# Semaphores between GpSimd and VectorE, 22 products of zeros, and a new written-out order in a windowed-attention and highway kernel

## The chip, the cores and the metric

The kernel runs on one core of one Trainium2 chip. The metric is the device time of one launch in microseconds (us). The kernel before was run three times: 172.64, 172.2 and 172.1 us, a median of 172.2. One more execution was recorded by the profiler; it is the source of every profile line.

## What is computed

Attention with a sliding window and a distance bias, over 8 batches, 8 heads, 576 positions and head size 64; its output is the input x of a highway layer of 4608 tokens by 512.

```python
scores = scale * np.matmul(q, k.transpose(0, 1, 3, 2))
bias = slopes[:, None, None] * (-np.abs(rel).astype(np.float32))[None, :, :]
mask = (rel >= 0) & (rel < window)                 # window = 128
scores = np.where(mask, scores + bias[None], -1000000000.0)
attn = softmax(scores); attn_out = np.matmul(attn, v)
H = np.maximum(x @ w_h, 0.0)
T = 1.0 / (1.0 + np.exp(-(x @ w_t + b_t)))
out = T * H + (1.0 - T) * x
```

## The kernel before, in words

**Stages.** Each batch has four stages of 128 positions; the last 64 positions of two batches make one more stage, so there are 36 of these "blocks". The attention weights are exp(score) times a table which holds exp(bias) inside the window and zero outside it. A column of ones beside v gives the sums. The gate is taken from tanh: T = 0.5 + 0.5 tanh(z / 2), and the output is T (H - x) + x.

**Order by hand.** The framework schedules nothing. A string, ORDER, lists steps of one letter and a two-digit number, and each engine gets its instructions in that order; a semaphore is waited for wherever data or a buffer demands it. The string is the output of a planner outside the kernel. The string BANKS gives, in the same order, the PSUM bank that each product takes. The letters that the text uses, with line and engine:

- L, V, W: loads of q or k (L128), of v (L134), of the weights wH and wT (L138) and the bias bT (L142). All are issued by GpSimd. L00 to L03 are batch 0's q and k, L04 to L07 batch 1's; V00 is batch 0's v. W00 is wH, W01 wT. Eight semaphores serve these loads in turn, so a load also waits until the eighth load before it has landed. There are two sets of q/k tiles: L08 overwrites what L00 brought, after the transpose T00.
- R, P, Q, A: clearing of tiles by VectorE (L152 to L170). S, r, k: the table, by GpSimd (L179, L181), VectorE (L185 to L189) and ScalarE (L194, L198). B: a copy of the bias to all partitions, issued by SyncE.
- T: transpose of a q or k tile, VectorE, L211. Four per batch are needed before its first scores.
- s: scores, TensorE, L239 and L249. e: exp, ScalarE, L263. m: product with the table ("the mask"), VectorE, L270.
- p, y, Y: weights times v, TensorE, L303 (Y drains TensorE first). n: normalisation, VectorE, a reciprocal (L312) and a product (L313).
- x, c: transpose on TensorE (L322) and copy on ScalarE (L327). h: product with w_h, TensorE, L332. z: product with w_t, TensorE, L359 and, for the bias, L363, or b, a copy of the bias by ScalarE (L350).
- u: ScalarE's relu (L342), followed by v, VectorE's H - x (L346); or U: both in one, VectorE (L338).
- a: tanh, ScalarE, L367. Then 0.5 + 0.5 t: t on ScalarE (L372) or D on VectorE (L374).
- the gate's product: G on GpSimd or g on VectorE (both L380). The sum with x: o on GpSimd or O on VectorE (both L385). d: store, issued by SyncE (L391, L395).

**VectorE's operations with two operands in SBUF** are m (L270), v (L346), g (L380) and O (L385); D (L374) has one, in 16 bits, input and output in SBUF. The text calls these five "with lock", because the change treats them alike. T, n and U are not among them: T has one operand, and the others read PSUM.

**Where GpSimd stands.** G and o wait for their data alone; the letter's place in ORDER decides what is before and behind it in GpSimd's own queue, but not how it stands against VectorE. In ORDER the list has, for example, "... m12 m13 m14 ... m15 ... G09 ..." : G09 is written behind the mask m15, but no semaphore says so.

The string before begins: R00 L00 L01 Q00 L02 L03 P00 S00 V00 r00 W00 T00 k00 W01 T01 W02 L04 T02 L05 L06 and so on.

Of the kernel before, what the change touches and what calls it, by code (L numbers as in the profile page):

```python
# [15 lines left out]
ORDER = (
    "R00L00L01Q00L02L03P00S00V00r00W00T00k00W01T01W02L04T02L05L06L07T03A00s00s01e00e01s02m00L"
    "08e02s03m01e03p00m02V01Y00p01n00Y01p02n01x00Y02c00x01n02h00L09c01m03x02z00U00c02T04h01a0"
    "0v00p03z01T05D00Y03G00a01T06z02t01o00h02T07a02L10d00U02u01s04B00n03G01e04T08s05L11e05s06"
    "L12m04L13e06x03m05p04Y04v02c03n04s07p05m06e07x04h03D02T09G02Y05c04p06T10L14U03Y06V02h04b"  # L20
    "03n05z03v03n06L15x05z04a03m07c05x06z05a04T11o01c06h05u04L16a05d01T12s08b06h06U05D05e08D0"
    "3v05z06T13G03p07U06s09m08L17a06Y07e09V03p08n07Y08n08x07s10L18c07m09x08e10h07T14o03p09c08"
    "p10u07Y09o02t04Y10n09b08h08G05t06d02n10d03x09z07c09v06L19U08m10L20z08a07L21g04s11v08a08g"
    "06D07x10T15o06e11z09O04V04h09g07c10d04s12D08m11U09z10e12T16o05h10a09G08s13a10d05u10d06p1"
    "1e13p12D10Y11v09o07Y12n11s14n12G10e14x11d07T17x12L22c11s15D09c12m12h11e15m13h12m14p13U11"
    "p14m15Y13b11p15Y14U12z11n13G09z12n14a11L23v11x13T18o08x14c13p16y15t11Y16v12L24d08a12z13n"
    "15o09c14b14n16x15h13a13G11d09T19t13h14c15o11T20z14U14L25h15D12u13a14L26s16D14V05T21U15z1"
    "5e16v14x16O10p17L27a15s17m16d10c16Y17d11e17D15h16G12n17p18b16u16G14s18T22Y18e18x17o12z16"
    "n18c17G13s19d12T23a16h17e19V06D16m17z17m18U17s20a17v15p19m19e20p20Y19Y20G15n19t17s21n20p"
    "21o13e21Y21T24x18o14x19d13c18s22n21c19h18L28e22d14m20h19m21U18s23v17b19x20T25G17e23z18T2"  # L30
    "6o15z19c20T27p22G16x21a18d15h20c21u19a19L29h21m22U20L30z20m23U21t19y22p23a20o17n22p24Y23"
    "p25n23Y24L31Y25G19n24p26x22x23n25c22z21o19c23T28x24o16y26a21h22T29c24b22V07d16x25h23d17D"
    "18c25n26t20z22v18U23v20s24u22a22h24e24g18D21v21z23g20v23b24O18s25a23D22z24d18m24U24d19e2"
    "5x26g22h25T30o20z25t23u25d20c26m25s26a24h26a25T31o22e26z26D24U26m26s27a26p27g21e27Y27g23"
    "p28o21n27Y28n28x27d21s28d22c27v24p29e28D25x28m27h27c28Y29m28U27s29g24h28b27v26e29n29o24z"
    "27u28p30t26g25s30m29a27Y30e30x29G26n30z28c29o23s31a28z29e31D28d23m30d24x30g28h29v27c30D2"
    "7m31p31a29p32Y31h30b30n31o26U29z30U30O25x31y32v29a30d25p33d26c31n32p34Y33t29p35D30v30x32"
    "g27h31c32n33G30h32O28z31g29U32u31o27b32y34a31y35n34x33o30d27z32c33d28n35x34z33a32O29t31D"
    "32d29x35c34g31h33d30v32g32z34O31U33a33O32d31h34c35v33d32a34D33z35g33t34u34h35O33a35g34d3"
    "3D35U35O34v35d34g35O35d35"  # L40
)
BANKS = (
    "4040640376304602504074065402435403401240240124176242014234024034012406123421036240124120"
    "4143142042014034021467106204673623104013401241042034023423042341024601520467636272034503"
)


# [22 lines left out]
def kernel(  # L70
# [74 lines left out]
    def pads(i):  # L145
        for g in range(NG):
            for w in "qk":
                nc.vector.memset(TR[i, g, w][:, S:SQ, :], 0.0)

    def clear(step):  # L150
        if step == "R":
            nc.vector.memset(ident[:], 1.0)  # L152
            nc.vector.memset(ones0[:], 0.0)
            nc.vector.memset(ones0[0:1, :], 1.0)
            nc.vector.memset(bT[:], 0.0)
            nc.vector.memset(VA[0][:, :, D : D + 1], 1.0)
            pads(0)
        elif step == "P":
            for p in PB:
                nc.vector.memset(p[:, :, 0:64], 0.0)  # L160
                nc.vector.memset(p[:, :, 256:320], 0.0)
                nc.vector.memset(p[:, :, 512:576], 0.0)
        elif step == "Q":
            for p in PE3:
                nc.vector.memset(p[:, :, 0:64], 0.0)
            nc.vector.memset(MK3[:, :, :, 192:256], 0.0)
# [36 lines left out]
    def additive():  # L203
        for h in range(NH):
            for g in range(NG):
                nc.gpsimd.tensor_scalar(
                    out=MA[:, h, g, :], in0=rel[:], scalar1=-slopes[4 * g + h] / scale,
                    scalar2=None, op0=ALU.mult)

    def tr(w, b, g):  # L210
        nc.vector.transpose(  # L211
            out=TR[b % 2, g, w][:, 0:S].rearrange("p s e -> p (s e)").bitcast(U32).rearrange(
                "p (s t) -> p t s", t=NT),
            in_=LD[b % 2, g, w][:].bitcast(U32).rearrange("p (t i) -> p t i", i=32))
# [52 lines left out]

    def mask(b, s):
        p = pview(b, s)
        nc.vector.tensor_tensor(out=p, in0=p, in1=(MK3 if s == 3 else MK)[:], op=ALU.mult)  # L270
# [46 lines left out]
    XP, XT, PA, PZ, TT, UU, OT = {}, {}, {}, {}, {}, {}, {}  # L317
# [25 lines left out]

    def sub_x(b, s):
        uu = UU[b, s][:]
        nc.vector.tensor_tensor(out=uu, in0=uu, in1=X[b, s][:], op=ALU.subtract)  # L346
# [22 lines left out]
    def to_gate(b, s, on):  # L369
        tt = TT[b, s]  # L370
        if on == "t":
            nc.scalar.activation(out=tt[:], in_=tt[:], func=ACTF.Copy, bias=0.5, scale=0.5)  # L372
        else:
            nc.vector.tensor_scalar(out=tt[:], in0=tt[:], scalar1=0.5, scalar2=0.5,  # L374
                                    op0=ALU.mult, op1=ALU.add)

    def gate(b, s, on):
        eng = nc.vector if on == "g" else nc.gpsimd
        uu = UU[b, s][:]
        eng.tensor_tensor(out=uu, in0=uu, in1=TT.pop((b, s))[:], op=ALU.mult)  # L380

    def add_x(b, s, on):
        eng = nc.gpsimd if on == "o" else nc.vector
        ot = OT[b, s] = ft.tile([P, DM], F32, name="ot")
        eng.tensor_tensor(out=ot[:], in0=UU.pop((b, s))[:], in1=X[b, s][:], op=ALU.add)  # L385
# [57 lines left out]
```

## Time and profile before

| what | value |
|---|---|
| median of three runs | 172.2 us (172.1 to 172.64) |
| the profiled execution, its own time | 172.49 us |
| its span, first to last instruction | 170.5 us |
| mean granted TensorE clock | 0.924 |
| PE / DVE / ACT / POOL busy | 135.1 / 152.8 / 119.3 / 94.0 us |
| GpSimd tensor operations | 18 gates (L380) and 25 sums (L385) |
| loads | 15.21 MB through GpSimd's queue, 81.9% of 16 engines' span |

In the lines to come, PE is TensorE, PEld its weight loads, DVE VectorE, ACT ScalarE, POOL GpSimd and SP SyncE. A group's line ends with busy us, mean ns of one, and idle time before it with what ended that. A timeline row begins with start and duration in us and covers several instructions where it ends in "x3". The slices cut the span into 40 parts and give the busy share in tenths. The granted clock is 1 at full speed.

### The profile page before, as it was taken

How to read it: one execution, taken by the hardware profiler on the slowest of the kernel's cores; microseconds unless marked ns; L12 is line 12 of the kernel's file. 1: busy time of each engine (PE TensorE's matmuls, PEld its weight loads, DVE VectorE, ACT ScalarE, POOL GpSimd, SP SyncE). 2: the span in 40 equal slices, each digit the busy share in tenths (PEclk: the TensorE clock that was granted, in tenths of full speed). 3: DMA queues.
4: the chain of work that ended last, by engine and by line, in shares of the span. 5: the costliest groups of instructions: out<-in, count | busy, mean ns of one | idle time of the engine just before them, and what ended most of it. 6: DMA issues, size and time to landing. Idle time of an engine off the chain costs nothing.

```text
span 170.5 us, 6188 instructions
## 1 busy us (share of the span) xinstructions
PE 135.1 (79%) x2696; PEld 73.8 (43%) x2696; DVE 152.8 (90%) x268; ACT 119.3 (70%) x172; POOL 94.0 (55%) x93
## 2 busy tenths in 40 slices
PE   0016999679998996899992899995999999999940
PEld 0014744434454443545450447443645555565410
DVE  7995699796889999999999987999999998899990
ACT  3199656952698796674883479991599999975740
POOL 7951508457089488690978619299609217318000
PEclk9999999755999999659999579999999999999997
DMA  3999999999989999968199891739495030333452
GB/s 55 198 157 198 211 205 160 217 203 148 190 156 137 234 230 136 262 93 188 18 158 169 218 123 62 139 79 186 107 159 171 25 127 4 125 110 139 161 212 62
DMA packets 48106, 25.30 MB, mean 148 GB/s; under 512 B 38224, under 2 KB 39248, under 8 KB 48080
## 3 DMA queue, kind: packets, MB, share of 16 engines
q0 software_dynamic: 42688, 15.21, 81.9%
q1 hardware_dynamic: 5392, 9.70, 15.9%
q8 instruction: 21, 0.34, 0.8%
q14 instruction: 5, 0.04, 0.1%
HBM read 30.67 MB, written 9.44 MB: 235 GB/s over the span
## 4 chain that ended last, share of the span: by engine, by line
DVE 43%; PE 24%; POOL 12%; issue 12%; ACT 6%; DVEq 0%; POOLq 0%; ACTq 0%
DVE p L270 7%; PE ps L303 6%; PE ps L359 6%; PE ps L332 6%; DVE x L313 5%; POOL ot L385 5%; DVE tt L374 4%; ACT p L263 4%; POOL uu L380 4%; DVE ot L385 3%; PE ps L322 3%; DVE uu L380 3%; PE ps L239 3%; DVE uu L346 2%; DVE uu L338 2%
## 5 line engine op out<-in xcount | busy, mean ns | idle before, releaser
L380 POOL TENSOR_TENSOR uu<-uu,tt 128x512 bf16<-128x512 bf16 x18 | 25.7, 1430 | 38.9 <-DVE tt L374 17.6
L385 POOL TENSOR_TENSOR ot<-uu,x 128x512 f32<-128x512 bf16 x25 | 33.4, 1346 | 15.9 <-DVE uu L380 12.2
L332 PE MATMUL ps<-wH,xt 128*128 128x512 bf16 x144 | 40.3, 412 | 0.0
L263 ACT ACTIVATE p<-ps 128x1536 bf16<-128x1536 f32 x24 | 34.5, 1455 | 7.4 <-PE ps L239 7.4
L359 PE MATMUL ps<-wT,xt 128*128 128x512 bf16 x144 | 37.8, 387 | 0.2 <-DVE x L313 0.2
L303 PE MATMUL ps<-va,p 64*128 64x65 bf16 x768 | 25.4, 204 | 9.5 <-DVE x L313 4.0
L270 DVE TENSOR_TENSOR p<-p,mk 128x1536 bf16<-128x1536 bf16 x24 | 28.7, 1211 | 2.5 <-ACT p L263 2.5
L367 ACT ACTIVATE tt<-ps 128x512 f16<-128x512 f32 x36 | 21.4, 602 | 11.6 <-PE ps L359 7.2
L327 ACT COPY xt<-ps 128x512 bf16<-128x512 bf16 x36 | 20.8, 586 | 10.0 <-PE ps L322 9.6
L303 PEld LDWEIGHTS <-p 64*128 64x128 bf16 x768 | 18.9, 102 | 19.7 <-issue 15.5
L313 DVE TENSOR_TENSOR x<-ps,rd 128x512 bf16<-128x512 f32 x36 | 24.9, 691 | 1.5
L332 PEld LDWEIGHTS <-xt 128*128 128x128 bf16 x144 | 13.4, 104 | 15.1 <-issue 3.9
L359 PEld LDWEIGHTS <-xt 128*128 128x128 bf16 x144 | 13.2, 100 | 14.1 <-issue 1.8
L342 ACT ACTIVATE uu<-ps 128x512 bf16<-128x512 f32 x24 | 14.4, 602 | 5.8 <-PE ps L332 5.4
L322 PE MATMUL ps<-ident,x 128*128 128x128 bf16 x144 | 15.2, 235 | 3.2 <-issue 1.2
L263 ACT ACTIVATE r<-ps 128x2048 bf16<-128x2048 f32 x8 | 15.0, 1876 | 2.1 <-PE ps L249 1.9
L239 PE MATMUL ps<-tr00q,tr00k 32*64 32x192 bf16 x256 | 7.1, 294 | 11.8 <-DVE tr00q L211 10.4
L134 POOL DMA_DIRECT2D va<-in_v_dram x8 | 15.0, 1873 | 1.4 <-DMA wH<-in_moe_w_h_dram 1.4
L374 DVE TENSOR_SCALAR tt<-tt 128x512 f16<-128x512 f16 x23 | 11.9, 521 | 2.4 <-ACT tt L367 2.4
L322 PEld LDWEIGHTS <-x 128*128 128x128 bf16 x144 | 9.7, 103 | 9.3 <-DVE x L313 3.7
L270 DVE TENSOR_TENSOR r<-r,mk 128x2048 bf16<-128x2048 bf16 x8 | 11.6, 1455 | 0.1
L346 DVE TENSOR_TENSOR uu<-uu,x 128x512 bf16<-128x512 bf16 x24 | 10.6, 446 | 0.7 <-ACT uu L342 0.7
(75 smaller groups left out, 192.1 us busy)
## 6 DMA issues: line engine op xcount, KB each, us to landing
out_dram<-ot SPq DMA_DIRECT2D x32, 256.0 KB, 2.5
va<-in_v_dram POOLq DMA_DIRECT2D x8, 576.0 KB, 9.9
ld00k<-in_k_dram POOLq DMA_DIRECT2D x4, 288.0 KB, 8.2
ld00q<-in_q_dram POOLq DMA_DIRECT2D x4, 288.0 KB, 5.0
ld01k<-in_k_dram POOLq DMA_DIRECT2D x4, 288.0 KB, 6.6
ld01q<-in_q_dram POOLq DMA_DIRECT2D x4, 288.0 KB, 7.2
ld10k<-in_k_dram POOLq DMA_DIRECT2D x4, 288.0 KB, 7.9
ld10q<-in_q_dram POOLq DMA_DIRECT2D x4, 288.0 KB, 8.9
```

The lines of the kernel that those rows point to most:

```text
L263: nc.scalar.activation(out=pview(b, s), in_=SC.pop((b, s))[:, :, 0:n].rearrange("p h (g n) -> p h g n", g=NG), func=ACTF.Exp, scale=scale)
L270: nc.vector.tensor_tensor(out=p, in0=p, in1=(MK3 if s == 3 else MK)[:], op=ALU.mult)
L303: mm = nc.tensor.matmul(out=av[o : o + m, par, j * (D + 1) : (j + 1) * (D + 1)], lhsT=PT[bb, st][rows, h, c : c + m], rhs=VA[bb][rows, at ...
L313: nc.vector.tensor_tensor(out=x[:].rearrange("p (i r d) -> p r i d", i=NH, r=2), in0=av[:, :, :, 0:D], in1=rd[:].to_broadcast([P, 2, NH, D ...
L322: nc.tensor.transpose(out=pt[:, c * P : (c + 1) * P], in_=X[b, s][:, c * P : (c + 1) * P], identity=ident[:])
L327: nc.scalar.copy(out=xt[:].rearrange("p c n -> p (c n)"), in_=XP.pop((b, s)))
L332: nc.tensor.matmul(out=pa, lhsT=XT[b, s][:, c, :], rhs=wH[:, c, :], start=c == 0, stop=c == NC - 1)
L359: nc.tensor.matmul(out=pz, lhsT=xt[:, c, :], rhs=wT[:, c, :], start=c == 0 and not given, stop=c == NC - 1 and given, skip_group_check=given)
L367: nc.scalar.activation(out=tt[:], in_=PZ.pop((b, s)), func=ACTF.Tanh, scale=0.5)
L374: nc.vector.tensor_scalar(out=tt[:], in0=tt[:], scalar1=0.5, scalar2=0.5, op0=ALU.mult, op1=ALU.add)
L380: eng.tensor_tensor(out=uu, in0=uu, in1=TT.pop((b, s))[:], op=ALU.mult)
L385: eng.tensor_tensor(out=ot[:], in0=UU.pop((b, s))[:], in1=X[b, s][:], op=ALU.add)
```

## The change

- GpSimd's G and o get one more semaphore: each waits for the last VectorE operation with lock that stands ahead of it in ORDER (`alone` notes it, `between` adds the wait). Loads that GpSimd issues get none.
- VectorE clears one more tile (J), and TensorE multiplies it with itself 22 times (K) ahead of its first scores, into a bank that the scores overwrite later.
- ORDER and BANKS are new. Counted by letter, VectorE's D goes from 23 to 19 and ScalarE's t from 13 to 17; GpSimd's G from 18 to 15 and VectorE's g from 18 to 21; GpSimd's o from 25 to 24 and VectorE's O from 11 to 12; the drains Y from 30 to 28. All other counts are the same.
- A helper that this kernel doesn't call (`additive`; ADD is empty) moves to ScalarE.

The new ORDER begins: R00 L00 B00 L01 P00 L02 L03 L04 S00 J00 Q00 K00 L05 A00 L06 L07 r00 V00 T00 k00 W00 T01 L08 T02 V01 T03 T04 s00 L09 s01 e00 W01 T05. Batch 1's loads now stand ahead of V00 and of both weights, and its four transposes T04 to T07 ahead of the first mask.

```diff
+SPIN = 22
 ORDER = (
-    "R00L00L01Q00L02L03P00S00V00r00W00T00k00W01T01W02L04T02L05L06L07T03A00s00s01e00e01s02m00L"
...
+    "R00L00B00L01P00L02L03L04S00J00Q00K00L05A00L06L07r00V00T00k00W00T01L08T02V01T03T04s00L09s"
...
+    spin = cp.tile([P, DM], BF16, name="spin")
     PS = pp.tile([P, 8, 512], F32, name="ps")
+
+    paired = [None]
+
+    def alone(ins):
+        paired[0] = ins.ins
+
+    def between(ins):
+        if paired[0] is not None:
+            tc.add_manual_dep(
+                ins.ins, paired[0].name,
+                mybir.DependencyInfo(mybir.DependencyClass.Sync, mybir.DependencyReason.DATA),
+                reason="starts behind VectorE's last operation with two SBUF operands")
...
+        if step == "J":
+            nc.vector.memset(spin[:], 0.0)
...
+    def warm():
+        ps = take(1)[:, 0, :]
+        for _ in range(SPIN):
+            nc.tensor.matmul(out=ps, lhsT=spin[:, 0:P], rhs=spin[:], start=True, stop=True)
...
-        nc.vector.tensor_tensor(out=p, in0=p, in1=(MK3 if s == 3 else MK)[:], op=ALU.mult)
+        alone(nc.vector.tensor_tensor(out=p, in0=p, in1=(MK3 if s == 3 else MK)[:], op=ALU.mult))
...
-        nc.vector.tensor_tensor(out=uu, in0=uu, in1=X[b, s][:], op=ALU.subtract)
+        alone(nc.vector.tensor_tensor(out=uu, in0=uu, in1=X[b, s][:], op=ALU.subtract))
...
-            nc.vector.tensor_scalar(out=tt[:], in0=tt[:], scalar1=0.5, scalar2=0.5,
-                                    op0=ALU.mult, op1=ALU.add)
+            alone(nc.vector.tensor_scalar(out=tt[:], in0=tt[:], scalar1=0.5, scalar2=0.5,
+                                          op0=ALU.mult, op1=ALU.add))
...
-        eng = nc.vector if on == "g" else nc.gpsimd
+        eng, note = (nc.vector, alone) if on == "g" else (nc.gpsimd, between)
         uu = UU[b, s][:]
-        eng.tensor_tensor(out=uu, in0=uu, in1=TT.pop((b, s))[:], op=ALU.mult)
+        note(eng.tensor_tensor(out=uu, in0=uu, in1=TT.pop((b, s))[:], op=ALU.mult))
...
-        eng = nc.gpsimd if on == "o" else nc.vector
+        eng, note = (nc.gpsimd, between) if on == "o" else (nc.vector, alone)
         ot = OT[b, s] = ft.tile([P, DM], F32, name="ot")
-        eng.tensor_tensor(out=ot[:], in0=UU.pop((b, s))[:], in1=X[b, s][:], op=ALU.add)
+        note(eng.tensor_tensor(out=ot[:], in0=UU.pop((b, s))[:], in1=X[b, s][:], op=ALU.add))
```

More of the change, by code (lines that the diff above doesn't have):

```diff
@@ L16 @@
 ORDER = (
-    "R00L00L01Q00L02L03P00S00V00r00W00T00k00W01T01W02L04T02L05L06L07T03A00s00s01e00e01s02m00L"
[L18 to L40, printed above, removed]
+    "R00L00B00L01P00L02L03L04S00J00Q00K00L05A00L06L07r00V00T00k00W00T01L08T02V01T03T04s00L09s"
@@ new lines @@
+    "01e00W01T05e01s02W02T06e02s03L10T07e03m00s04m01e04s05m02L11e05m03p00p01Y00m04p02n00Y01L1"
+    "2x00n01Y02c00p03L13n02x01h00c01T08s06U00y03e06x02n03h01m05x03c02L14s07c03u01h02e07m06L15"
+    "h03T09U02p04m07p05U03p06Y04Y05n04V02z00v00n05x04p07T10L16c04y06Y07a00z01n06b03t00n07z02a"
+    "01G00T11x05x06L17c05h04T12a02L18s08c06o00u04z03e08v02d00z04v03D01b06T13G01s09a03h05a04T1"
+    "4L19e09h06o01T15z05U05L20d01U06v05V03D04s10D02a05m08p08e10z06m09L21x07Y08D05c07g02s11D03"
+    "a06n08G04h07e11T16G05x08z07u07L22c08m10s12a07p09e12v06Y09o02p10n09Y10o04s13n10d02p11e13T"
@@ new lines @@
+    "17x09G03x10Y11T18c09s14o03c10h08e14n11L23h09d03D06d04V04m11U08s15b08x11m12e15z08m13z09m1"
+    "4U09z10a08T19o05c11p12a09p13m15L24d05Y12t09L25h10b11v08t08n12G06h11a10u10t07z11U11O06p14"
+    "a11G07y13d06p15n13Y14p16Y15o07n14Y16x12n15p17G08c12d07x13n16Y17c13x14o08x15n17c14h12c15v"
+    "09h13t10d08D11g09U12s16T20o09b14z12e16u13L26d09h14T21V05a12s17U14T22z13e17L27m16z14V06a1"
+    "3v11s18g10a14v12p18D13e18x16v14z15m17c16g13s19m18a15h15e19T23o10y18h16n18L28d10U15L29s20"
+    "g11L30T24b16p19o11e20Y19z16n19o13d11t14x17T25p20c17L31Y20a16u16s21G14t12x18n20e21z17V07D"
@@ new lines @@
+    "15g12x19v15c18x20m19h17a17c19z18m20U17c20s22T26o12b19h18e22T27o14d12z19d13U18s23m21d14a1"
+    "8h19m22e23z20u19D18a19D16p21m23p22a20p23Y21t17Y22n21t20h20g15p24n22U20o15y23Y24n23p25x21"
+    "G16d15Y25c21n24x22z21c22v17T28o16t19p26a21x23n25G17h21d16c23b22x24g19x25c24y26o19z22U21n"
+    "26c25h22v18t21g18a22x26O17z23c26v20d17v21s24u22G21h23e24T29o18h24T30U23s25a23d18h25m24b2"
+    "4d19U24z24D22e25u25g20z25v23D23a24T31o20s26a25h26e26m25d20z26D24U26m26s27a26g22p27e27v24"
+    "Y27o22p28n27Y28o21n28x27s28c27p29m27e28d21x28d22h27D25c28s29m28Y29e29g23h28n29o23U27s30u"
@@ L41 @@
+    "28d23b27p30g24x29m29e30z27O24Y30c29s31d24n30a27z28e31v26D27g25x30v27z29m30a28g27c30h29m3"
+    "1p31p32U29p33o27Y31b30Y32n31a29z30t29D26D28x31n32G26p34a30y33c31Y34n33G28t30p35x32n34h30"
+    "c32O26x33x34c33y35v29h31O25c34U30g29d25z31d26v30b32d27n35G30z32a31u31x35t31O29h32c35O28a"
+    "32h33g31d28U32O30d29z33U33v32d30O31t32z34a33v33d31g32t33h34O32a34g33d32h35t34o33u34z35U3"
+    "5g34d33v35O34a35d34D35g35O35d35"
 )
 BANKS = (
-    "4040640376304602504074065402435403401240240124176242014234024034012406123421036240124120"
@@ L44 @@
-    "4143142042014034021467106204673623104013401241042034023423042341024601520467636272034503"
+    "4404040642160504570672407624750460460547047074506406540540567124076026504536506740504670"
+    "6706404067540607405642064621305436541705604570450646046706074606752306234130354701726326"
+    "0"
 )
@@ L150, in clear @@
     def clear(step):
-        if step == "R":
+        if step == "J":
+            nc.vector.memset(spin[:], 0.0)
+        elif step == "R":
             nc.vector.memset(ident[:], 1.0)
@@ L205, in additive @@
             for g in range(NG):
-                nc.gpsimd.tensor_scalar(
-                    out=MA[:, h, g, :], in0=rel[:], scalar1=-slopes[4 * g + h] / scale,
-                    scalar2=None, op0=ALU.mult)
+                nc.scalar.activation(out=MA[:, h, g, :], in_=rel[:], func=ACTF.Copy,
+                                     scale=-slopes[4 * g + h] / scale)
     def tr(w, b, g):
@@ L405 @@
                 continue
-            if step in "RPQA":
+            if step == "K":
+                warm()
+                continue
+            if step in "JRPQA":
                 clear(step)
```

## The prediction

> **What bounds the kernel now.** I read the page first: busy shares, the slices and the chain.
>
> ```profile
> PE 135.1 (79%) x2696; PEld 73.8 (43%) x2696; DVE 152.8 (90%) x268; ACT 119.3 (70%) x172; POOL 94.0 (55%) x93
> DVE  7995699796889999999999987999999998899990
> PEclk9999999755999999659999579999999999999997
> DVE 43%; PE 24%; POOL 12%; issue 12%; ACT 6%; DVEq 0%; POOLq 0%; ACTq 0%
> ```
>
> VectorE (DVE) is busy 152.8 of 170.5 us, almost without a hole from the fourth tenth on, and holds 43% of the chain. TensorE (PE) comes second. Its clock is about halved in three places (the 5s and the 6). So a microsecond less on VectorE shortens the run until TensorE is late.
>
> How much of the 152.8 us is work? The answers by source line give minimum/median/maximum, the groups by form give means:
>
> ```profile
> L270 DVE TENSOR_TENSOR p<-p,mk x24: 930/955/2861, 14.6 to 146.6; 128x1536 bf16<-128x1536 bf16 x24
> L270 DVE TENSOR_TENSOR r<-r,mk x8: 1211/1218/2171, 22.0 to 148.3; 128x2048 bf16<-128x2048 bf16 x8
> L374 DVE TENSOR_SCALAR tt<-tt x23: 277/288/1500, 25.7 to 163.8; 128x512 f16<-128x512 f16 x23
> L346 DVE TENSOR_TENSOR uu<-uu,x x24: 403/418/868, 24.3 to 164.6; 128x512 bf16<-128x512 bf16 x24
> L380 DVE TENSOR_TENSOR uu<-uu,tt x18: 405/418/1375, 59.0 to 165.1; 128x512 bf16<-128x512 bf16 x18
> L385 DVE TENSOR_TENSOR ot<-uu,x x11: 658/684/799, 61.3 to 165.6; 128x512 f32<-128x512 bf16 x11
> ...
> L270 DVE TENSOR_TENSOR p<-p,mk 128x1536 bf16<-128x1536 bf16 x24 | 28.7, 1211 | 2.5 <-ACT p L263 2.5
> L374 DVE TENSOR_SCALAR tt<-tt 128x512 f16<-128x512 f16 x23 | 11.9, 521 | 2.4 <-ACT tt L367 2.4
> L270 DVE TENSOR_TENSOR r<-r,mk 128x2048 bf16<-128x2048 bf16 x8 | 11.6, 1455 | 0.1
> L346 DVE TENSOR_TENSOR uu<-uu,x 128x512 bf16<-128x512 bf16 x24 | 10.6, 446 | 0.7 <-ACT uu L342 0.7
> L380 DVE TENSOR_TENSOR uu<-uu,tt 128x512 bf16<-128x512 bf16 x18 | 9.4, 524 | 0.1
> ```
>
> Mean minus median, times count: 24 x 256 ns = 6.1; 8 x 237 = 1.9; 23 x 233 = 5.4; 24 x 28 = 0.7; 18 x 106 = 1.9. Together **16.1 us** in which VectorE stood inside an instruction. GpSimd (POOL) beside it shows why:
>
> ```profile
> 71.52 1.78 POOL L380 TENSOR_TENSOR uu<-uu,tt 128x512 bf16<-128x512 bf16 x1 [1.67 <-DVE tt L374]
> 73.86 1.26 POOL L385 TENSOR_TENSOR ot<-uu,x 128x512 f32<-128x512 bf16 x1
> 75.67 1.28 POOL L385 TENSOR_TENSOR ot<-uu,x 128x512 f32<-128x512 bf16 x1
> ...
> 71.35 4.59 DVE L270 TENSOR_TENSOR p<-p,mk 128x1536 bf16<-128x1536 bf16 x3
> 75.86 2.17 DVE L270 TENSOR_TENSOR r<-r,mk 128x2048 bf16<-128x2048 bf16 x1
> ```
>
> Three masks took 4.59 us (three medians: 2.87) and the fourth 2.17 (median 1.22), while three GpSimd operations ran. In the order list these three (G09, o08, o09) stand behind m15, v11 and v12, that is, behind all four masks. They had their data and started up to 6.5 us ahead of their place. Going through all lengthened VectorE operations in the timeline, I find 17 beside GpSimd tensor operations, and in each the GpSimd operation stood later in the list than it ran; those that ran on time lengthened nothing. Two more stood beside a load that GpSimd was issuing, and end with it:
>
> ```profile
> 84.77 1.85 POOL L134 DMA_DIRECT2D va<-in_v_dram  x1
> 85.23 1.50 DVE L374 TENSOR_SCALAR tt<-tt 128x512 f16<-128x512 f16 x1
> ...
> 61.31 1.87 POOL L134 DMA_DIRECT2D va<-in_v_dram  x1
> 61.94 1.38 DVE L380 TENSOR_TENSOR uu<-uu,tt 128x512 bf16<-128x512 bf16 x1
> ```
>
> They cost 1.21 + 0.96 = 2.2 us; the tensor operations therefore 16.1 - 2.2 = **13.9 us**.
>
> **The change, part by part.** The profiled run took 172.49 us, 0.3 above the median of 172.2; its span is 170.5. I sum against 172.5.
>
> *The waits: -13.9.* A GpSimd tensor operation can no longer start ahead of the VectorE operation before it in the list, so the early kind goes. What is left: walking the new list, I add up the VectorE operations without lock that follow each of the 39 GpSimd operations, against about 1.15 us of one. In 34 cases these cover it (two transposes, or two normalisations); five are short by 0.06, 0.31, 0.06, 0.31 and 0.55 us: **+1.3**. A GpSimd operation can also come late, where several stand behind one VectorE operation or behind an issue. One such case costs up to a whole one (0.95 us for a mask above). None to five are possible; I take one: **+1.0**. Behind a waiting operation in GpSimd's queue stand the next loads, and whoever transposes them. GpSimd has room: 94.0 us busy, and it loses four operations.
>
> *Issues are not covered.* In the new list V03 stands right before two L374 operations, V04 right behind one, V07 right before one. Zero to three meetings at 1.2 us against 2.2 us now: -2.2 to +1.4, taken as 0.
>
> The Trainium skill, "SBUF — State Buffer", section "SBUF: two separate sides", calls the shared port pair an exclusive lock which the one that starts first keeps for the whole instruction. The 17 cases agree. It adds that two SBUF inputs alone meet only a GpSimd operation that reads SBUF; by that the 1.38 us at 61.94 should not have been, so here the row decides.
>
> *Work moved between engines: +1.0.* VectorE gives four L374 to ScalarE (-4 x 0.29), takes three gates (3 x 0.42) and one sum (0.68) from GpSimd, and clears one more tile (0.27, as the row below). ScalarE gets 4 x 0.63 = 2.5 us on 119.3, which its idle time takes.
>
> ```profile
> L166 DVE MEMSET mk<- 128x256 uint32 x1 | 0.3, 272 | 0.0
> L372 ACT ACTIVATE tt<-tt 128x512 f16<-128x512 f16 x13 | 8.2, 631 | 0.1
> 10.36 0.55 PE L239 MATMUL ps<-tr00q,tr00k 32*64 32x192 bf16 x16 [10.36 <-DVE tr00q L211]
> 96.69 1.71 PE ps L359 x4
> 100.94 0.86 PE ps L359 x4
> ```
>
> *The 22 products: 0.* TensorE idles for its first 10.36 us. At the slow clock four products of 512 columns take 1.71 us, so 22 take 9.4, at the fast clock (0.86) 4.7. They can start once their tile is cleared, some 4.5 us in, and end between 9.2 and 13.9. The scores need four transposes, done at about 12.5 now. So the products are covered, or late by 1.4 at most. Their worth is a fast clock for the first scores; but those are paced by the loads, below, so between 0 and -1.4, and I take 0.
>
> *The order at the front: -3.0.* It moves the four q/k loads of batch 1 ahead of V00 and the weights. From issue to landing:
>
> ```profile
> ld01q<-in_q_dram POOLq DMA_DIRECT2D x1, 288.0 KB, 6.9
> ld11q<-in_q_dram POOLq DMA_DIRECT2D x1, 288.0 KB, 15.1
> va<-in_v_dram POOLq DMA_DIRECT2D x1, 576.0 KB, 10.6
> wT<-in_moe_w_t_dram POOLq DMA_DIRECT2D x1, 512.0 KB, 12.3
> ...
> 3.09 0.55 POOL L128 DMA_DIRECT2D ld01q<-in_q_dram  x1
> 4.68 1.96 POOL L134 DMA_DIRECT2D va<-in_v_dram  x1
> 7.38 0.76 POOL L138 DMA_DIRECT2D wT<-in_moe_w_t_dram  x1
> 22.74 1.03 PE L359 MATMUL ps<-wT,xt 128*128 128x512 bf16 x4
> ```
>
> Now the fourth load lands at 10.0, V00 at 15.3, wT at 19.7: they land one behind the other. Put in the new order at these gaps (q/k 1.45, v 5, a weight 2.2), V00 lands at about 21 and wT, now behind V00, wH, L08, V01 and L09, at about 34. The first gate product moves from 22.7 to 34: +11.3 at worst. Against it, VectorE gets four transposes and two masks early:
>
> ```profile
> 13.00:45.00 32.00, 26.82 (x528) 15.68 (x513) 25.93 (x41) 20.64 (x24) 14.29 (x16) 0.84 1.47 189
> 45.00:100.00 55.00, 46.87 (x950) 24.65 (x948) 52.49 (x73) 39.21 (x54) 37.85 (x33) 0.88 1.22 169
> 100.00:165.00 65.00, 60.33 (x1197) 32.53 (x1195) 61.64 (x110) 53.31 (x77) 32.37 (x25) 1.00 0.55 117
> ```
>
> (Columns: window, length, busy of PE, PEld, DVE, ACT, POOL, clock, DMA.) VectorE idles 6.1 us between 13 and 45, the most that can be won. Bounds -6.1 and +11.3; I take half the idle time, since VectorE is the engine that ends last and it has work without wT.
>
> *TensorE gives back: +2.5.* Behind 100 us TensorE is busy 60.3 of 65.0, so hardly more than 4.7 us can go there. Of the 13.9 us about 5 lie there (the masks at 113 and 116 alone are 2.9). I let half pass.
>
> *The clock: -1.4.* Between 45 and 100 it averages 0.88. The L359 group at 96.69 took 1.71 us and the one behind it 0.86; two such groups on the chain cost some 1.4 us, and with VectorE quicker TensorE waits less there.
>
> Sum: 172.5 - 13.9 + 1.3 + 1.0 + 1.0 - 3.0 + 2.5 - 1.4 = 160.0; against the median, 0.3 less: **159.7**.
>
> **The rivals.**
>
> *TensorE becomes the bound, 167.* If nothing passes behind 100 us and half between 45 and 100, the waits win 13.9 - 5 - 4.5 = 4.4, less 1.0 for moved work, and the front -1.5: 167.3. For it: 60.3 of 65. Against it: chain and slices show VectorE.
>
> *The front starves the gates, 174: slower.* If all behind the first gate product follows wT and moves by 11.3 us, against 13.9 - 1.3 - 1.0 - 1.0 - 2.5 + 1.4 = 9.5 won, the run takes 174.0 after the 0.3. It decides if the sixth L359 group, at 44.9 now, comes after 54. Against it: now three of the six run before 28 and the next only at 42.5, so there is slack behind the first.
>
> *The collisions stay, 171.* If GpSimd mostly comes late, it meets the next locked operation instead: 172.5 + 1.0 - 3.0 = 170.5, or about unchanged.
>
> *The clock falls again.* In 13 to 45 it averaged 0.84 although TensorE was busy 26.8 of 32. With V00 at 21 the scores after the products run thin, and a second slow stretch of ten microseconds at half speed costs at most 5: 164.7 when it all reaches the end. The Trainium skill, "TensorE: Matmul & The Clock Gate", section "Part 1: The HAM clock gate", says an idle window of about 3.4 us brings the half clock back. By that rule, the products' worth would be gone before V00 lands.
>
> **How the numbers follow.** Forecast (150.8 to 165): 0.50; the falling clock, 164.7: 0.10. TensorE: 0.14. Collisions stay: 0.08, half of it within 0.3%, about what a measurement of this kernel can tell from no change. Front: 0.18, slower. So faster 0.78, same 0.04, slower 0.18. The low end takes all 6.1 us at the front and lets TensorE pass all: 172.5 - 13.9 + 1.0 - 6.1 - 1.4 - 0.3 = 151.8, less 1.0 of issue meetings: 150.8. The high end, 173.5, takes in all but the worse part of the front.
>
> **What would show it.** Right: VectorE means at their medians (masks near 0.96, L374 near 0.29), VectorE busy near 138, GpSimd operations starting right behind VectorE ones, V00's first use near 21, the first L359 group near 34 but the sixth before 46. Wrong: lengthened masks beside GpSimd operations, now late ones; the sixth L359 behind 54; TensorE with gaps and a clock under 0.8 up to 45; loads queued behind waiting GpSimd operations and transposes idle for them.

## The result and the profile after

| | before | after |
|---|---|---|
| median, all runs | 172.15 us (171.47 to 172.64, 4 runs) | 162.16 us (161.11 to 162.92, 4 runs) |
| ratio after / before | | 0.9418 [0.9353, 0.9484] |
| profiled execution, own time / span | 172.49 / 170.5 us | 162.92 / 161.1 us |
| mean granted TensorE clock | 0.924 | 0.939 |

The change is 10.0 us faster, where 12.5 was forecast (159.7). Ratios here and below leave out a kernel's slow executions (over 1.5% above its fastest), so they differ a little from the quotients of the medians given. The page of after: busy times, VectorE's slices, the clock, the chain.

```profile
PE 135.3 (84%) x2718; PEld 73.7 (46%) x2718; DVE 140.5 (87%) x269; ACT 121.2 (75%) x176; POOL 79.6 (49%) x89
DVE  7899956698999999757899999899899999889980
PEclk9998555999999997799999999999999999999996
PE 68%; ACT 13%; DVE 10%; issue 5%
```

VectorE is 12.3 us less busy, TensorE the same. The chain now lies on TensorE (68%, was 24%) instead of VectorE (10%, was 43%). A slowed clock shows in two places only (the 5s and the 7s), but the first lies early, in the fifth to seventh slice. The clock row counts the time ahead of the trace's first record of the clock as full speed, and it isn't: before the change, matmuls run at the slow clock up to about 21.9 us (sixteen scores in 0.55 us where they take 0.38 later, rows under old_products), though the row of before has 9s there.

The answers by line of after, masks and D (minimum/median/maximum):

```profile
L291 DVE TENSOR_TENSOR p<-p,mk x24: 931/946/1086, 17.7 to 136.4; 128x1536 bf16<-128x1536 bf16 x24
L291 DVE TENSOR_TENSOR r<-r,mk x8: 1206/1218/1509, 20.3 to 137.6; 128x2048 bf16<-128x2048 bf16 x8
L395 DVE TENSOR_SCALAR tt<-tt x19: 266/284/1683, 45.0 to 155.1; 128x512 f16<-128x512 f16 x19
```

The medians are those of before; the maxima of the masks fell from 2861 and 2171 ns to 1086 and 1509. Only D still has one that is several times its median. Here is how a GpSimd pair now starts (timeline, VectorE's row, then GpSimd's):

```profile
53.08 0.28 DVE L395 TENSOR_SCALAR tt<-tt 128x512 f16<-128x512 f16 x1
...
53.45 2.27 POOL L401 TENSOR_TENSOR uu<-uu,tt 128x512 bf16<-128x512 bf16 x2 [2.33 <-DVE tt L395]
```

GpSimd stood idle for 2.33 us, and began 0.09 us after the end of D (53.08 + 0.28). Every one of the 39 does: none starts sooner than 0.08 us behind its VectorE operation. Added up over the trace as excess over each group's median, VectorE's lengthening beside GpSimd tensor operations fell from 14.1 us (17 cases) to 1.2 (6 cases).

Where the time went, as VectorE's windows show it (columns as in the prediction):

```profile
13.00:45.00 32.00, 25.13 (x597) 15.49 (x597) 26.87 (x40) 22.38 (x28) 10.81 (x15) 0.79 1.68 188
45.00:100.00 55.00, 50.16 (x1074) 26.68 (x1073) 49.77 (x83) 45.95 (x64) 38.75 (x38) 0.97 1.32 174
100.00:155.60 55.60, 52.97 (x1011) 28.62 (x1011) 51.48 (x101) 47.73 (x71) 19.57 (x18) 1.00 0.52 127
```

The span fell by 9.4 us: VectorE's busy time by 12.3, while its idle time rose by 2.9 (17.7 to 20.6). By window the idle time went from 6.1 to 5.1 up to 45, from 2.5 to 5.2 between 45 and 100, and from 3.4 to 4.1 behind 100 (up to 5.5 us ahead of the end). So part of the gain was given back, and in the middle.

### The profile page after: what moved, and what is told of

It is laid out like the page before. It is cut to its first block, busy times and chain, and to the rows that moved or that the text cites. A ratio compares the mean times of both kernels' runs of the same rounds, so it can differ in the third digit from the quotient of the medians.

```text
span 161.1 us, 6240 instructions
## 1 busy us (share of the span) xinstructions
PE 135.3 (84%) x2718; PEld 73.7 (46%) x2718; DVE 140.5 (87%) x269; ACT 121.2 (75%) x176; POOL 79.6 (49%) x89
## 3 DMA queue, kind: packets, MB, share of 16 engines
q1 hardware_dynamic: 5392, 9.70, 17.7%
## 4 chain that ended last, share of the span: by engine, by line
PE 68%; ACT 13%; DVE 10%; issue 5%
PE ps L353 19%; PE ps L380 18%; PE ps L324 13%; PE ps L260 8%; PE ps L343 7%; ACT p L284 6%; PE ps L384 3%; ACT mk L211 3%; ACT r L284 2%; DVE tt L395 2%; DVE x L334 1%; DVE p L291 1%; DVE over L204 1%; ACT tt L388 1%; PE ps L270 1%
## 5 line engine op out<-in xcount | busy, mean ns | idle before, releaser
L406 POOL TENSOR_TENSOR ot<-uu,x 128x512 f32<-128x512 bf16 x24 | 27.6, 1157 | 36.6 <-DVE uu L401 16.1
L353 PE MATMUL ps<-wH,xt 128*128 128x512 bf16 x144 | 37.8, 396 | 0.0
L380 PE MATMUL ps<-wT,xt 128*128 128x512 bf16 x144 | 36.6, 380 | 0.0
L348 ACT COPY xt<-ps 128x512 bf16<-128x512 bf16 x36 | 20.7, 588 | 13.2 <-PE ps L343 12.5
L401 POOL TENSOR_TENSOR uu<-uu,tt 128x512 bf16<-128x512 bf16 x15 | 17.2, 1153 | 19.4 <-DVE uu L367 8.1
L324 PE MATMUL ps<-va,p 64*128 64x65 bf16 x768 | 23.3, 197 | 4.1 <-issue 1.1
L291 DVE TENSOR_TENSOR p<-p,mk 128x1536 bf16<-128x1536 bf16 x24 | 22.5, 956 | 0.1
L353 PEld LDWEIGHTS <-xt 128*128 128x128 bf16 x144 | 13.0, 101 | 14.1 <-issue 3.2
L380 PEld LDWEIGHTS <-xt 128*128 128x128 bf16 x144 | 12.9, 98 | 13.6 <-issue 0.5
L333 DVE RECIPROCAL rd<-ps 128x8 f32<-128x8 f32 x36 | 7.2, 200 | 9.3 <-PE ps L324 9.2
L343 PE MATMUL ps<-ident,x 128*128 128x128 bf16 x144 | 13.5, 225 | 1.2 <-DVE x L334 1.1
L291 DVE TENSOR_TENSOR r<-r,mk 128x2048 bf16<-128x2048 bf16 x8 | 10.0, 1252 | 1.9 <-ACT r L284 1.9
L393 ACT ACTIVATE tt<-tt 128x512 f16<-128x512 f16 x17 | 10.6, 631 | 0.2
L235 PE MATMUL ps<-spin 128*128 128x512 bf16 x22 | 6.7, 477 | 4.5 <-DVE spin L167 4.5
```

What stands on the lines that cost most here:

```text
L291: alone(nc.vector.tensor_tensor(out=p, in0=p, in1=(MK3 if s == 3 else MK)[:], op=ALU.mult))
L324: mm = nc.tensor.matmul(out=av[o : o + m, par, j * (D + 1) : (j + 1) * (D + 1)], lhsT=PT[bb, st][rows, h, c : c + m], rhs=VA[bb][rows, at ...
L343: nc.tensor.transpose(out=pt[:, c * P : (c + 1) * P], in_=X[b, s][:, c * P : (c + 1) * P], identity=ident[:])
L348: nc.scalar.copy(out=xt[:].rearrange("p c n -> p (c n)"), in_=XP.pop((b, s)))
L353: nc.tensor.matmul(out=pa, lhsT=XT[b, s][:, c, :], rhs=wH[:, c, :], start=c == 0, stop=c == NC - 1)
L380: nc.tensor.matmul(out=pz, lhsT=xt[:, c, :], rhs=wT[:, c, :], start=c == 0 and not given, stop=c == NC - 1 and given, skip_group_check=given)
```

## Experiments

The theory from the prediction (W in what was expected): the waits carry the gain, because VectorE's lengthened operations vanish. The first rival (O): the new order and the products carry it. The kernel before was timed on the same chips; its medians in the three sets were 170.52, 171.88 and 171.53 us. Repeats of one kernel spread by 1 to 3%, so less than one per cent between two kernels is not read.

### The parts of the change, one by one

**old_waits**: the kernel before, its order untouched, no products, with the semaphores alone.

```diff
 (kernel before)
+        alone(...)      # around m, v, D, g, O, as in the change
+        between(...)    # around G, o, as in the change
```

> The order before with the new semaphores alone. Theory W (the waits carry the gain): VectorE loses its 13.9 us beside GpSimd tensor operations, masks go to a mean near 960 ns, and the time falls by 8 to 12 us, to 160 to 164. Rival O (the new order carries it): the old order, written for a GpSimd that runs ahead, stalls at the waits; time within 3 us of 172, with GpSimd or its loads late instead.

Measured: 164.43 us, ratio 0.9597 [0.9526, 0.9668], a fall of 6.1 us, less than the 8 to 12 of theory W. The masks by line (of an execution of 167.81 us):

```profile
L290 DVE TENSOR_TENSOR p<-p,mk x24: 926/947/1053, 14.5 to 141.1; 128x1536 bf16<-128x1536 bf16 x24
L290 DVE TENSOR_TENSOR r<-r,mk x8: 1206/1214/1226, 21.9 to 142.9; 128x2048 bf16<-128x2048 bf16 x8
```

The long ones are gone (maxima 1053 and 1226), without any new order. The lengthening beside GpSimd tensor operations is 1.9 us instead of 14.1. The first rival falls: the semaphores alone win 4.0% of the 5.8%.

**new_nowaits**: the new order and the products, without the semaphores.

```diff
-        if paired[0] is not None:
+        if False:
```

> The changed kernel without the semaphores. Theory W: GpSimd runs ahead again, the mean mask goes back over 1100 ns and the time to 170 to 174. Rival O: collisions cost little in this order, 162 to 165.

Measured: 169.24 us, ratio 0.9919 [0.9873, 0.9964]. The lengthening is back: 11.6 us in 14 cases, the mean mask 1132 ns. Its timeline, VectorE and then GpSimd:

```profile
58.14 2.17 DVE L291 TENSOR_TENSOR p<-p,mk 128x1536 bf16<-128x1536 bf16 x1
60.23 1.37 DVE L367 TENSOR_TENSOR uu<-uu,x 128x512 bf16<-128x512 bf16 x1
...
58.33 1.15 POOL L401 TENSOR_TENSOR uu<-uu,tt 128x512 bf16<-128x512 bf16 x1
59.56 1.76 POOL L406 TENSOR_TENSOR ot<-uu,x 128x512 f32<-128x512 bf16 x1
```

A mask that takes 0.95 alone took 2.17, and GpSimd's gate ran inside it (58.33 to 59.48). Then GpSimd's sum took 1.76 instead of 1.15 beside the end of the mask and the difference, which took 1.37 instead of some 0.4. So the mechanism is shown from both sides: the semaphores give 4.0% in the old order and 5.0% in the new. The order with its products gives 0.8% without them, which is too little to be read, and 1.8% with them (0.9597 to 0.9418, intervals that barely part).

**new_noproducts**: the change without J and K. **old_products**: the kernel before with J and K, and no semaphores. Of ORDER the first line is shown; the rest moves along, and BANKS loses or gains the products' bank.

```diff
 (new_noproducts)
-    "R00L00B00L01P00L02L03L04S00J00Q00K00L05A00L06L07r00V00T00k00W00T01L08T02V01T03T04s00L09s"
+    "R00L00B00L01P00L02L03L04S00Q00L05A00L06L07r00V00T00k00W00T01L08T02V01T03T04s00L09s01e00W"
 (old_products)
-    "R00L00L01Q00L02L03P00S00V00r00W00T00k00W01T01W02L04T02L05L06L07T03A00s00s01e00e01s02m00L"
+    "R00L00L01Q00L02L03J00P00K00S00V00r00W00T00k00W01T01W02L04T02L05L06L07T03A00s00s01e00e01s"
```

> The changed kernel without the 22 products of zeros and the clearing of their tile. As predicted (worth 0 to 1.4 us): 162 to 163.6, since V00 lands at 20.6 either way and the clock falls again at 15. Rival: the products carry several microseconds, 165 or more.

> The kernel before with the 22 products ahead of its first scores, nothing else. Its scores, first weights-times-v and first two h and z groups ran at the slow clock up to 21.9 us. Theory that the products are worth nothing in themselves: 171.5 to 172.5. Rival: a fast clock from the first scores on wins 2 to 4 us here, where V00 lands at 15 and TensorE is on the chain from 17 on: 168 to 170.

Measured: new_noproducts 163.09 us, ratio 0.948 [0.941, 0.9551]: its interval overlaps with that of the whole change. old_products 173.84 us, ratio 1.0243 [1.0181, 1.0304]: slower, which no theory had. TensorE's timeline before, then in old_products:

```profile
12.52 0.55 PE L239 MATMUL ps<-tr01q,tr01k 32*64 32x192 bf16 x16 [1.61 <-DVE tr01q L211]
...
17.32 2.48 PE L303 MATMUL ps<-va,p 64*128 64x65 bf16 x64
```

```profile
12.43 0.38 PE L260 MATMUL ps<-tr01q,tr01k 32*64 32x192 bf16 x16 [1.78 <-DVE tr01q L227]
14.41 0.55 PE L260 MATMUL ps<-tr00q,tr00k 32*64 32x192 bf16 x16 [1.26 <-ACT p L284]
...
20.58 0.40 PE L324 MATMUL ps<-va,p 64*128 64x65 bf16 x8 [1.21 <-issue]
24.72 1.91 PE L380 MATMUL ps<-wT,xt 128*128 128x512 bf16 x4
```

The products do make the first scores quick (0.38 against 0.55 for sixteen), but those start at the same time, 12.43 against 12.52: they are paced by the loads and transposes. By 14.41 the clock is down again. Then the weights-times-v group meets a stop of 1.21 us that it didn't have, and the first gate product, at 24.72, runs at the slow clock (1.91) where before it ran at 22.74 in 1.03. A warm-up ahead of thin work bought nothing and moved the later return of the fast clock; how much of the 2.4% is the clock and how much the stop was not separated. In the new order the products are worth nothing that can be measured, either way.

**new_34**: 34 products instead of 22, so that TensorE is busy until the scores.

```diff
-SPIN = 22
+SPIN = 34
```

> The changed kernel with 34 products in place of 22. Theory F: TensorE's stops without a named cause (1.56 us at 22.5, 0.92 at 34.9, 1.97 at 62.5) come where it runs out of fetched instructions, every 256 instructions (numbers 450, 962, 1986 in its program): the stops stay at these numbers, so they come 12 matmuls earlier in the work. Rival: they belong to the work itself (the scores blocks they fall in) and stay with it. Time: within 1 us of the changed kernel, ratio 0.936 to 0.948; the products end near 13.9, beside the last transpose that the scores need.

Measured: 163.15 us, ratio 0.9551 [0.9454, 0.9647], outside the 0.936 to 0.948 expected. No gain; the interval overlaps with that of the change. The scores now run at the fast clock up to 20.3 us, about when V00 lands, and the first gate product still comes at 37.2 (37.1 in the change). On the stops, theory F holds. The first one of after lies behind 9 of 16 tr11q scores (row at 22.47, further down); here it lies behind 13 of the 16 tr10q scores that precede them, exactly 12 matmuls earlier:

```profile
22.49 0.37 PE L260 MATMUL ps<-tr10q,tr10k 32*64 32x192 bf16 x3 [0.68 <-issue]
```

### Is TensorE the bound now?

The chain says TensorE (theory P); VectorE, still busy 87%, is the rival (V). For both halves together the theories are that each engine hides the other's gain (C), or that neither's amount of work sets the time (L). Three kernels leave work out: half of the terms of h (144 products to 72), the mask on half of the heads, or both; old_halfh does the first to the kernel before.

```diff
 (halfh)
-        for c in range(NC):
+        for c in range(2):
...
-                             start=c == 0, stop=c == NC - 1)
+                             start=c == 0, stop=c == 1)
 (halfmask)
-        alone(nc.vector.tensor_tensor(out=p, in0=p, in1=(MK3 if s == 3 else MK)[:], op=ALU.mult))
+        alone(nc.vector.tensor_tensor(out=p[:, 0:2], in0=p[:, 0:2], in1=(MK3 if s == 3 else MK)[:, 0:2], op=ALU.mult))
```

> The changed kernel with half of its first product left out (two of the four 128-row parts of x @ w_h, 72 matmuls of 0.216 us = 15.5 us of TensorE). Theory P (the changed kernel ends with TensorE, which holds 68% of its chain): 7 to 12 us less than the changed kernel, a ratio of 0.87 to 0.90 to the kernel before. Rival V (VectorE, busy 140.5 of 161.1, still sets the end): at most 3 us less, 0.925 or more.

> The kernel before with the same half left out. Theory P says that there VectorE with its collisions sets the end, TensorE little: 0 to 4 us less, ratio 0.975 to 1. If TensorE set the end before as well: 0.95 or less.

> The changed kernel with the mask applied to half of the heads only (the other half of each 128x1536 or 128x2048 product is left out: about 24 x 0.40 + 8 x 0.53 = 14 us of VectorE). Theory P: 0 to 4 us less than the changed kernel, ratio 0.92 to 0.942. Rival V: 7 to 13 us less, 0.865 to 0.90.

> The changed kernel with both halves left out at once: half of x @ w_h (15.5 us of TensorE) and the mask on half of the heads (about 14 us of VectorE). Alone, neither moved the time (ratios 0.945 and 0.946 against 0.942). Theory C (TensorE and VectorE end within a few us of each other, and each hides what the other saves): now 7 us or more less, ratio 0.90 or lower. Rival L (something else, the loads of the front or ScalarE or the slow clock, sets it): 0.93 or more.

| kernel | median us | ratio to before |
|---|---|---|
| new_halfh | 163.7 | 0.9448 [0.9325, 0.9572] |
| old_halfh | 171.0 | 0.9988 [0.9856, 1.0119] |
| new_halfmask | 162.27 | 0.9459 [0.9371, 0.9546] |
| new_half_both | 162.05 | 0.9499 [0.941, 0.9588] |

The busy lines of new_halfh, new_halfmask and new_half_both, and VectorE's longest wait (total, times, longest) in new_half_both and then in after:

```profile
PE 126.9 (78%) x2646; PEld 69.9 (43%) x2646; DVE 140.9 (86%) x269; ACT 120.0 (73%) x176; POOL 79.7 (49%) x89
```

```profile
PE 134.3 (84%) x2718; PEld 73.2 (46%) x2718; DVE 128.6 (81%) x269; ACT 120.9 (76%) x176; POOL 79.7 (50%) x89
```

```profile
PE 119.4 (75%) x2616; PEld 67.7 (43%) x2646; DVE 128.4 (81%) x269; ACT 119.6 (75%) x176; POOL 79.7 (50%) x89
```

```profile
DVE rd L333 <- PE ps L324: 14.1, 17, 2.7
```

```profile
DVE rd L333 <- PE ps L324: 9.2, 13, 1.8
```

Before, halving h changed nothing that can be read, as expected where VectorE sets the end; that test isn't clean, since in its trace VectorE's lengthening grew as well (17.2 us where it was 14.1). After the change, neither halving shortens the run, and both together don't either: with 12 us less on VectorE and up to 16 less on TensorE (30 of 2646 matmul records are missing there) the time is that of the change. In new_half_both VectorE only waits longer for the weights-times-v products: 14.1 us, in after 9.2. So "TensorE is now the bound", which the chain's 68% suggests, is not right as a statement of amounts, and neither is "each hides the other". Which chain of latencies through loads, TensorE, ScalarE (120 us busy in all four) and VectorE sets what is left was not settled. In new_halfh alone TensorE's busy time fell by 8.4 us only, not by the 15.5 that was expected, with a granted clock of 0.887 instead of 0.939; so that kernel by itself says less than its edit suggests. Two rivals stand untested. The last load lands at 109 to 112 us in all four (129.4 before the change), so halving work didn't bring the loads forward. Behind it ScalarE may set the pace: between 113 and 153 us of new_half_both it is busy 36.0 of 40.0 us, more than VectorE (35.4) and TensorE (33.7).

### The order at the front, and the issues

**new_ones_later**: A (clearing the columns of ones, a step of VectorE ahead of the first transposes) moved behind the third.

```diff
-    "R00L00B00L01P00L02L03L04S00J00Q00K00L05A00L06L07r00V00T00k00W00T01L08T02V01T03T04s00L09s"
+    "R00L00B00L01P00L02L03L04S00J00Q00K00L05L06L07r00V00T00k00W00T01L08T02A00V01T03T04s00L09s"
```

> The changed kernel with one step moved: the seven clearings of the columns of ones (A00) behind the third transpose instead of ahead of the table's step r00. In the changed kernel V00's issue (6.82 to 8.69) held an operation of r00 for 1.36 us, and the first transpose starts at 9.08; here r00 is past before V00's issue, and the first transpose should start near 7.3, the first exp near 12.3 instead of 14.1. Theory that the front's chain (table, exps, scores) sets the whole: 1 to 2 us less, ratio 0.93 to 0.937. Rival: V00, which lands at 20.6 either way, sets it: no change, 0.94 to 0.945.

Measured: 161.84 us, ratio 0.943 [0.9358, 0.9502], the same as the change; the first transpose began at 6.9 us instead of 9.1 and the first gate product came at 36.6 instead of 37.1. Nothing is won by earlier transposes.

**new_vwaits**: GpSimd's issue of a v load gets the semaphore too, and V03 moves behind two D.

```diff
-    "4L19e09h06o01T15z05U05L20d01U06v05V03D04s10D02a05m08p08e10z06m09L21x07Y08D05c07g02s11D03"
+    "4L19e09h06o01T15z05U05L20d01U06v05D04s10D02V03a05m08p08e10z06m09L21x07Y08D05c07g02s11D03"
...
-            nc.gpsimd.dma_start(
+            between(nc.gpsimd.dma_start(
...
```

> The changed kernel with the extra semaphore on the issues of v as well, and V03 listed behind the L374 operations D04 and D02 instead of ahead of them. If issues of v hold L374 (1.68 us at 49.0 in the changed kernel) and not the masks, the held 1.4 us goes and no mask is lengthened by an issue. Time: 0 to 1.5 us less (0.933 to 0.943) if VectorE's microseconds still count at 49, no change if TensorE ends last there. Slower if the later loads of v starve TensorE.

The pair that it was aimed at, in after (GpSimd's issue, VectorE's two D):

```profile
48.74 1.83 POOL L149 DMA_DIRECT2D va<-in_v_dram  x1
...
49.01 1.88 DVE L395 TENSOR_SCALAR tt<-tt 128x512 f16<-128x512 f16 x2
```

and in new_vwaits, there and at a later v load:

```profile
49.53 0.49 DVE L395 TENSOR_SCALAR tt<-tt 128x512 f16<-128x512 f16 x2
49.93 1.82 DVE L291 TENSOR_TENSOR p<-p,mk 128x1536 bf16<-128x1536 bf16 x2
...
50.33 1.83 POOL L149 DMA_DIRECT2D va<-in_v_dram  x1 [1.04 <-DVE tt L395]
...
85.58 1.83 POOL L149 DMA_DIRECT2D va<-in_v_dram  x1 [0.85 <-DVE p L291]
...
85.86 0.41 DVE L367 TENSOR_TENSOR uu<-uu,x 128x512 bf16<-128x512 bf16 x1
86.19 1.31 DVE L395 TENSOR_SCALAR tt<-tt 128x512 f16<-128x512 f16 x1
```

The two D took 0.49 us instead of 1.88: the hold is gone there. But the delayed issue at 85.58 met another D, which was held for 1.31. The time: 163.9 us, ratio 0.958 [0.9479, 0.9681]; no gain, if anything a loss (its interval just touches that of the change). Beside the same issues, the masks at 49.93 (0.9 each) and the difference at 85.86 kept their usual times.

**new_comb**: new_34, new_ones_later and new_vwaits together (their edits are above).

> Together: A00 behind the third transpose, 34 products, the semaphore on the issues of v with V03 moved. If the parts add: 1 to 3 us less than the changed kernel, ratio 0.925 to 0.937. If the front is set by the landing of V01 and wT (29.6 and 33.0) and the rest by both engines, no change: 0.938 to 0.946.

Measured in five rounds: 164.97 us, ratio 0.9668 [0.9596, 0.974]: slower than the change. No version tried beats it.

## Why the prediction was right, and where its sizes were wrong

- **The waits, -13.9 + 1.3 + 1.0 = -11.6: right.** Measured in the traces: 14.1 to 1.2, so -12.9. Of the 2.3 us that were to stay, 1.2 did. The expected late case is there, though small: a gate of VectorE started 0.66 us after a GpSimd operation and took 0.77 instead of 0.42.

```profile
111.30 1.15 POOL L401 TENSOR_TENSOR uu<-uu,tt 128x512 bf16<-128x512 bf16 x1
...
111.96 0.77 DVE L401 TENSOR_TENSOR uu<-uu,tt 128x512 bf16<-128x512 bf16 x1
```

- **Issues, 0: about right.** 2.17 us before, 1.68 after, of which 1.40 in the one meeting at 49.01, which the prediction named (V03 ahead of two D). Its reading of the gate at 61.94 as held by an issue stands alone: in the 14 traces 110 masks, differences, gates and sums ran beside a v load's issue and no GpSimd tensor operation, and none was held (at most 0.01 us over its median). That gate also met a GpSimd sum that began at 63.20; in old_waits the same gate, beside an issue but not that sum, took 0.41 us. So the 0.96 us belongs more likely with the tensor operations.
- **Moved work, +1.0: right.** Four D less, three gates, a sum and a clearing more, at the medians: -4 x 0.284 + 3 x 0.416 + 0.684 + 0.27 = +1.07.
- **The 22 products, 0: right here.** Nothing that can be measured. That they can cost 2.4% was not foreseen (the bounds were 0 to -1.4): in the old order they do.
- **The order at the front, -3.0: the first step that failed.** VectorE's idle time from 13 to 45 fell by 0.9 only. It had waited 2.5 us for exponentials ahead of its masks there, and that wait is gone; but its wait for weights-times-v products grew from 3.1 to 4.8 us, nearly all of the 5.1 us idle that are left. The prediction took it that VectorE has work without wT, and left out that it needs V00's products. The rows of these and of the gate:

```profile
22.79 1.33 PE L324 MATMUL ps<-va,p 64*128 64x65 bf16 x32
...
37.11 1.04 PE L380 MATMUL ps<-wT,xt 128*128 128x512 bf16 x4
...
47.99 1.03 PE L380 MATMUL ps<-wT,xt 128*128 128x512 bf16 x4
```

V00 landed at 20.6 and wT at 33.0, close to the forecast (21 and 34), but V00 was first used at 22.79, the first gate group came at 37.1 (forecast 34) and the sixth at 48.0 (forecast before 46; before the change 44.9). So the starving of the gates is real, only its point (54) wasn't reached. Ahead of V00's use TensorE had slowed down and stopped:

```profile
13.97 0.38 PE L260 MATMUL ps<-tr01q,tr01k 32*64 32x192 bf16 x16
15.60 0.55 PE L260 MATMUL ps<-tr00q,tr00k 32*64 32x192 bf16 x16 [1.26 <-ACT p L284]
...
22.47 0.38 PE L260 MATMUL ps<-tr11q,tr11k 32*64 32x192 bf16 x7 [1.56 <-issue]
```

Sixteen scores take 0.38 up to 13.97 and 0.55 from 15.60; in the matmuls' durations the slow clock lasts until 28.7. This is the rival of the falling clock: the fast clock was gone before V00 landed. The rule that the prediction cites from the Trainium skill ("TensorE: Matmul & The Clock Gate", section "Part 1: The HAM clock gate") fits if a thin window counts as an idle one: from 11.6 to 15.0, ahead of the fall, TensorE was busy 0.96 of 3.40 us.

But neither the slow clock nor that stop is what holds the gates. Without the products, V00 is used at once:

```profile
21.16 2.48 PE L323 MATMUL ps<-va,p 64*128 64x65 bf16 x64 [1.42 <-DMA va<-in_v_dram]
...
29.83 0.19 PE L323 MATMUL ps<-va,p 64*128 64x65 bf16 x1 [1.85 <-issue]
```

The stop has moved to 29.83, the first gate product still comes at 37.5, and VectorE idles 5.7 us in the window. Counted by durations, from 13 to 45 TensorE runs at the slow clock for some 17 us in new_noproducts, 13.7 in the change and 10 in new_34, with no difference in time that can be read. Once wT has landed at 33.0, TensorE still has eight products of h and 64 of weights times v ahead of the gate in its list; what a front without any stop would take is not shown.

- **TensorE gives back, +2.5: size near by luck, place wrong.** It was to come behind 100 us, where TensorE is nearly full. VectorE's idle time grew by 0.8 there and by 2.7 between 45 and 100, where one place explains it, the window from 60 to 76, before and after:

```profile
60.00:76.00 16.00, 13.68 (x278) 7.02 (x273) 15.84 (x21) 12.43 (x15) 13.53 (x12) 0.80 1.21 181
```

```profile
60.00:76.00 16.00, 13.77 (x254) 6.93 (x252) 12.03 (x20) 11.43 (x18) 9.23 (x10) 0.89 1.23 174
```

VectorE was busy 15.84 of 16 and is busy 12.03. The rows of after tell how (TensorE, then ScalarE, then VectorE):

```profile
62.55 0.37 PE L260 MATMUL ps<-tr10q,tr10k 32*64 32x192 bf16 x14 [1.97 <-issue]
63.15 3.40 PE L353 MATMUL ps<-wH,xt 128*128 128x512 bf16 x8
...
66.96 0.24 PE L270 MATMUL ps<-tr10q,tr10k 32*128 32x64 bf16 x8
...
67.43 1.89 PE L380 MATMUL ps<-wT,xt 128*128 128x512 bf16 x8
...
67.32 1.88 ACT L284 ACTIVATE r<-ps 128x2048 bf16<-128x2048 f32 x1 [0.97 <-PE ps L270]
...
69.23 1.23 DVE L291 TENSOR_TENSOR r<-r,mk 128x2048 bf16<-128x2048 bf16 x1 [1.94 <-ACT r L284]
```

TensorE stopped for 1.97 us, then eight products of h took 3.40 at the slow clock (the like group of eight at 67.43 takes 1.89 at the fast one). The scores behind them in its order came late, so did the exponential, and VectorE idled for 1.94 us. In new_34, whose 12 further products move TensorE's instructions along, the same places read:

```profile
61.00 0.33 PE L324 MATMUL ps<-va,p 64*128 64x65 bf16 x10 [1.04 <-issue]
...
67.92 1.23 DVE L291 TENSOR_TENSOR r<-r,mk 128x2048 bf16<-128x2048 bf16 x1 [0.44 <-ACT r L284]
```

The stop is 1.04 and VectorE's wait 0.44. Yet new_34 is no faster, so this place explains where the idle time stands, not what sets the end.

- **The clock, -1.4: the direction right, the worth not shown.** Between 45 and 100 it rose from 0.88 to 0.97 as forecast, but VectorE's idle time there grew. From 13 to 45 the column reads 0.84 before and 0.79 after. That is no fall, and the prediction's 0.84 was a misreading: with the slow start up to 21.9 counted, TensorE was at the slow clock for some 19 of the 32 us before and 13.7 after.
- **The sum.** VectorE's busy time was to fall by 10.6 (11.6 less 1.0) and fell by 12.3. Its idle time was to change by -3.0 + 2.5 - 1.4 = -1.9 and rose by 2.9. So the direction came from the waits, and two errors partly cancel: VectorE's busy time fell by 1.7 us more than summed, its idle time came out 4.8 us higher, at the front and in the middle. That leaves 3.1 us of the span, 2.5 of the medians, so the nearness of the forecast is in part luck.
- **The rivals.** "Collisions stay" is refuted by the traces. "TensorE becomes the bound" is what the chain says, but the halved kernels speak against it.

## What to carry to other kernels

When the mean of an operation stands well above its median, look in the timeline at what ran beside the long ones; if it always ran ahead of its written place, one semaphore that keeps it there can pay, and it can be tried in the old order before any new order is made. Don't count VectorE's freed microseconds as time won: here 12.2 freed us (14.1 - 1.9) in the old order gave 6.1 us of the median, since other waits take their place (VectorE's wait for weights times v went from 4.4 to 9.6 us). Don't expect a gain from a warm-up of TensorE ahead of thin work: in the old order it cost 2.4%, in the new it did nothing.

## What the runs showed beyond this

**TensorE stops at fixed instruction numbers.** Its stops of 0.4 us and more that end by "issue" lie, in the traces with all matmul records to count by (after, new_halfmask, new_ones_later, new_halfh), at TensorE instructions 450, 962, 1986, 2498, 3266 and 3778, to within one: that is 194 plus a multiple of 256. The kernel before has one at 962 too (1.21 us, ended at 36.89). Not each kernel stops at each number. The page of after lists a queue that fits:

```profile
q8 instruction: 21, 0.34, 0.9%
```

21 packets, 0.34 MB: 16 KB each. One of them ran from 60.2 to 61.1, ahead of the stop that ended at 62.55; at each of the three stops of after, a packet ends 1.4 to 1.5 us before TensorE goes on. The Trainium skill, "Runtime: NRT & Kernel Launch", section "Instruction fetch mechanics", says that each engine's instructions are refilled in 16 KiB blocks of 256 and that the cost is mostly hidden. The spacing agrees; the cost isn't hidden here, with stops up to 2.75 us (in new_comb, ended at 61.73). new_34 rules out that the stops belong to the work in which they fall: with 12 more products ahead, the first came 12 matmuls earlier in it, at the same number. That fetching is their cause is argued from the numbers and the packets; no run here moved the fetch alone.

**A v load's issue holds D.** The 1.8 us issue held a 16-bit D by 1.0 to 1.4 us (85.23 before, 49.01 after, 86.19 in new_vwaits), while the masks beside one took about 0.9 each, as always. Over the 14 traces 29 of 35 D beside such an issue were held by more than 0.1 us, and none of the 110 operations with two operands. Delaying the issue moved the hold to another D.
